# Chunked attention and Fourier mix: the first batch's scores and exponentials in halves of the queries, and a newly planned order

## The chip, the cores and the metric

The kernel runs on one core of a Trainium2 chip. The metric is the device time of one execution in microseconds; what counts is the median over runs. Five engines work in parallel, each through its own instructions in order: PE (TensorE, matrix products), DVE (VectorE), ACT (ScalarE), POOL (GpSimd) and SP (SyncE, which only issues transfers here). POOL and ACT issue transfers too. PE writes to PSUM, a small memory of eight banks of 2 KB per partition; ScalarE and VectorE read it from there.

## The reference

```python
# q, k, v: (4, 8, 768, 64); mem_k, mem_v: (4, 8, 8, 64); w_ch1: (512, 2048); w_ch2: (2048, 512)
chunk, left_ctx, right_ctx = (32, 16, 8)
for c in range(nc):                        # 24 chunks of 32 queries
    c_start = c * chunk
    c_end = c_start + chunk
    l_start = max(0, c_start - left_ctx)
    r_end = min(S, c_end + right_ctx)
    k_full = np.concatenate([mem_k, k_ctx], axis=2)      # memory and keys l_start..r_end
    v_full = np.concatenate([mem_v, v_ctx], axis=2)
    scores = scale * np.matmul(q_c, k_full.transpose(0, 1, 3, 2))
    scores = scores - np.max(scores, axis=-1, keepdims=True)
    a = np.exp(scores)
    a = a / (np.sum(a, axis=-1, keepdims=True) + 1e-09)
    out[:, :, c_start:c_end] = np.matmul(a, v_full)
# x: the heads side by side, (4, 768, 512)
X = np.fft.fft(x, axis=1)
X = np.fft.fft(X, axis=2)
u = x + np.real(X).astype(np.float32)
un = (u - mu) / np.sqrt(var + 1e-06)       # over the last axis
ch = np.maximum(un @ w_ch1, 0.0) @ w_ch2
return (u + ch).astype(np.float32)
```

## The kernel before

The work goes by batch, four in all, and in each batch by pairs of heads, four pairs (n = 0 to 15 over the kernel, n = 0 to 3 in the first batch).

**Attention of a pair.** POOL issues the loads of q and k (`e_load_qk`, L356, into three buffers each), SP those of v (`e_load_v`, L368, four buffers `va`). PE turns q and k so that the head's dimension lies on the partitions (`e_turn_q`, `e_turn_k`, both through `turn`, L389 to L394); ACT copies q (`e_qT`), DVE or ACT copies k (`e_kT`) into a window of 96 keys for each tile of 64 queries: eight memory keys and 88 of the sequence, enough for both chunks of 32 queries in the tile. The two chunks, the halves, see different keys, so the exponential is taken once for each half with its own bias column of `mbias`, which masks the others (`e_masks`, L321).

For the first eight pairs scores come in two groups g of six tiles. `e_scores` (L442) writes 12 matmuls, six tiles by two heads, to a PSUM tile `sc` of two banks, one for each head. `e_exp` (L453) reads it with two activations, one for each half. There is one such tile (`sc=1` in the plan), so the next group's scores come after both. `e_values` (L489) multiplies by v, 24 matmuls a group, and `e_norm` (L505) divides by the sum on DVE. Pairs from n = 8 take all 24 score matmuls in one go (`a_scores`, L463) with two further banks, and pairs 4 to 7 use `e_scores` with the two exponentials as separate tasks.

**After attention.** The first batch has its own Fourier stage (`first_fourier`, L1211), which works as the values of the pairs come in; the others use `fourier`. A DFT along the sequence (`g_row`, `g_rows`, `e_rows`), one along the columns (`e_columns`, `h_columns`, `e_last_row`), sums and statistics on DVE, the normalised rows on ACT (`e_un`), and the two layers (`e_ch1`, `e_relu`, `e_ch2`, `e_prod`) follow. The tables of sines and cosines are computed in the kernel's first 14 us (`e_sines`, from angles on DVE), then ACT loads the exponential table (L1191). Until the first Fourier matrices are ready, PE's free time is filled with matmuls on zeros (`e_fill`, L1002, "idle" in the profile).

**The order.** Everything is added as a task (`add`, L57) with an engine, a cost, predecessors (`after`, `behind`), buffers that it takes and gives, and a rank. `Plan.order` (L106) plays the tasks in time: whenever an engine is free, the task of lowest rank that can start is placed. The instructions are emitted in the order of placement, and that fixes each engine's queue. Waits between engines come from the tiles' accesses, not from the plan's times. Without a given rank, a task's rank is its number. A table `moved` (L1547) overrides ranks by task number; its entries are numbers from a search. `WARM` is the time up to which the plan counts PE's tasks double, `FILL` the length of a filler. Task numbers follow the order of the `add` calls: 20 and 21 are the memsets of `kTb` (L1011), 32 is DVE's second step of the D angles (L1028), 36 the turn of the memory keys (L1160), 38 to 45 the loads, turns and copies of pair 0.

Of the kernel before, what the change touches and what calls it, by code (L numbers as in the profile page):

```python
# [37 lines left out]
class Plan:  # L38
# [7 lines left out]
    WARM = 6.0  # L46
# [3 lines left out]
    FILL = 0.215  # L50
    filling, fill = None, None
# [5 lines left out]
    def add(self, engine, cost, emit, after=(), take=(), give=(), rank=None, moved=0.0,  # L57
            loose=False, late=0.0, filler=False, behind=None, lag=0.0, pick=None, grain=0.1, head=1.0, dense=0.15):
        t = dict(engine=engine, cost=cost, emit=emit, after=[a for a in after if a is not None],
                 take=take, give=give, rank=len(self.tasks) if rank is None else rank,  # L60
                 moved=moved, done=None, at=None, no=len(self.tasks), loose=loose,
                 late=late, filler=filler, behind=behind, lag=lag, picks=[pick] if pick else [], grain=grain, head=head, dense=dense)
        self.tasks.append(t)
        return t
# [41 lines left out]
    def order(self):  # L106
        now, idle = 0.0, {}
# [8 lines left out]
        while any(waiting.values()):  # L116
# [5 lines left out]
            for e, ts_ in waiting.items():  # L122
# [3 lines left out]
                for t in ts_:  # L126
# [29 lines left out]
                    cost = t["cost"] * (2.0 if e == "PE" and now < self.WARM else 1.0)  # L156
                    idle[e] = t["end"] = now + cost - (0.0 if t["moved"] else self.OVER.get(e, 0.0))
# [38 lines left out]
def kernel(  # L196
# [11 lines left out]
    nc = tc.nc  # L208
# [64 lines left out]
    plan = Plan(dict(qs=NS, ks=NS, va=NV, kTb=NKT, kU=NKU, qT=2, tr=1, sc=1, xa=1, e1=3,  # L273
# [168 lines left out]
    def e_scores(n, g):  # L442
        qT, kT = qT_of[n], kTb[n % NKT]
        sc_of[n, g] = sc = aps.tile([P, 2, 8, 64], FP32, tag="sc", bufs=1, name="sc")
        for t6 in range(6):
            t = 6 * g + t6
            for hh in range(2):
# [3 lines left out]
                                 tile_position=(r0, 0))  # L451

# [524 lines left out]
    t_table = add("ACT", 1.55, lambda: nc.scalar.activation(warm, zero, AFT.Sin), [t_zero], rank=-3)  # L977
    t_iota = add("POOL", 0.7, e_iota, rank=-5)
    t_mkf = add("ACT", 1.3, e_mkf, moved=2.04, grain=0.077)
    t_id = add("POOL", 0.7, lambda: make_identity(nc, ident), rank=-1.5)  # L980
    t_scales = add("DVE", 0.2, e_scales, [t_iota], rank=-19)
    t_ones = {}
    def e_idb():
# [5 lines left out]
    t_idb = add("DVE", 0.5, e_idb, [t_id], rank=-16.5)  # L989
    t_kz = add("DVE", 0.5, lambda: nc.vector.memset(ks[0][QP:KP], 0.0), rank=-16.95)  # L990
    t_kzs = add("POOL", 2.0, lambda: [nc.gpsimd.memset(ks[i][QP:KP], 0.0) for i in range(1, NS)],
                rank=14)
    for i in range(NV):
        e_ = add("DVE" if i < 2 else "POOL", 0.68, lambda i=i: e_edges(i),
                 rank=(-20, -17.3, 17, 17)[i])
        t_ones[i] = add("POOL", 0.7, lambda i=i: e_edge_ones(i), [e_], rank=(-3.5, 2, 17.1, 17.1)[i])
    t_masks = add("POOL", 0.86, e_masks, rank=16)
# [13 lines left out]
    t_kTz = [add("POOL", 0.45, lambda i=i: nc.gpsimd.memset(kTb[i][:, :, KEYS:P], 0.0), rank=3)  # L1011
# [8 lines left out]
    for nm, parts, y, r, NN, c in (("S", tabS, yS.rearrange(fl3), rS.rearrange(fl3), S, 1.36),  # L1020
                                   ("D", tabD, yD.rearrange(fl2), rD.rearrange(fl2), DM, 0.77)):

        t1 = [add("DVE", 0.5, lambda p_=p_: nc.vector.tensor_scalar(
            p_[0], p_[2], p_[4], FSC, ALU.mult, ALU.add), [t_scales], rank=ANG[nm] + 0.1 * i)
            for i, p_ in enumerate(parts)]
        t2 = add("DVE", 0.95 if nm == "S" else 0.6, lambda y=y, NN=NN: nc.vector.tensor_scalar(
            y, y, FSC, float(NN), ALU.subtract, ALU.mult), t1, rank=ANG[nm] + 1)
# [18 lines left out]
    def attention(n):  # L1046
# [28 lines left out]
        else:  # L1075
            tq = (add("PE", 0.46 if first else 0.56, lambda: e_turn_q(n), [lq, t_idb], take=("tr",), give=("qs",))
# [5 lines left out]
            if n in JOINED:  # L1082
                tk, ktag = tq, pick_of.setdefault(("k", n), dict(of=("mlp", "acc")))
                tk["after"] += [lq, lk]
                tk["cost"] += 0.81
# [3 lines left out]
            else:  # L1089
                tk = add("PE", 0.48 if first else 0.56, lambda: e_turn_k(n), [lk, t_idb, t_kz if n == 0 else t_kzs],  # L1090
# [6 lines left out]
        if whole:  # L1097
            sp_ = pick_of["s", n] = dict(of=("mlp", "acc"))
            s_ = add("PE", 0.52, lambda: a_scores(n), [eq, ek, t_val[n - 1]], take=("sc", "tr"), pick=sp_, give=("qT", "kTb"))
        for g in range(2):  # L1100
            if whole:
                t_used["kTb", n % NKT] = t_sc[n, g] = s_
                for part in range(2):
# [4 lines left out]
                                           give=((), ("sc",), ("tr",), (sp_,))[2 * g + part])  # L1108
                    xs_.append(x_)
            else:  # L1110
                s_ = add("PE", 0.30 if first else 0.37, lambda g=g: e_scores(n, g), [eq, ek], take=("sc",),
                         give=("qT", "kTb") if g == 1 else (),
                         behind=t_sc.get((n, 0)))
                t_used["kTb", n % NKT] = s_
                t_sc[n, g] = s_
                x_ = None
                for halves in ((0, 1),) if first else ((0,), (1,)):
                    t_exp[n, g] = x_ = add("ACT", 1.05 if first else 0.58,
# [3 lines left out]
                                           give=("sc",) if 1 in halves else ())  # L1122
# [4 lines left out]
            if not first:  # L1127
                vp = dict(of=("mlp", "acc"))
                pick_of["v", n] = vp
                v_ = t_val[n] = add("PE", 1.64, lambda: [e_values(n, i) for i in range(2)]  # L1130
                                    + [x(n + 2) for x in (e_turn_q, e_turn_k) if n + 2 in JOINED],
                         xs_ + [lv], take=("xa",), pick=vp, give=("e1", "e1", "va"))
# [7 lines left out]
            v_ = add("PE", 0.85, lambda g=g: e_values(n, g), [x_, lv], take=(tag,),  # L1140
# [50 lines left out]
    add("ACT", 1.4, lambda: nc.scalar.activation(warm, zero, AFT.Exp), [t_sines], rank=SINES)  # L1191
    t_neg = add("DVE", 0.6, e_negatives, [t_sines], rank=100)
    t_rows = add("DVE", 1.6, e_table_rows, [t_sines, t_neg], rank=101)
# [126 lines left out]
    def columns_of(b, t_rest):  # L1320
# [21 lines left out]
        def columns(kt):  # L1342
            if b > 0 and kt > 2:
                if kt == 3:
                    cols[kt] = add("PE", 0.75, lambda: e_last_row(b), [t_sum[0]])
                return
            if b >= HALVED:
                cols[kt] = add("PE", 0.58, lambda: h_columns(b, kt), allr + t_mir_ + [cols.get(kt - 1)], take=("acc",),
# [8 lines left out]
            cols[kt] = add("PE", 0.9, lambda: e_columns(b, kt),  # L1357
# [237 lines left out]
```

## Time and profile before

| what | value |
|---|---|
| median of 3 runs | 276.81 us (276.75 to 277.06) |
| the profiled execution | 276.94 us |
| its span, first to last instruction | 275.2 us |
| instructions | 8215 |
| mean granted TensorE clock | 1.000 |
| scores of groups, first batch (L449), 15.50 to 34.60 us | 96 matmuls, 2.79 us busy |
| values, first batch (L501), same stretch | 192 matmuls, 7.28 us busy |
| turns of q and k (L393), same stretch | 80 matmuls, 2.68 us busy |
| exponentials (L459), 15 to 36 us | 16 activations of 96x384, 574 ns median |
| HBM read and written | 37.36 MB, 13.37 MB |

The page's utilization by slices shows how the engines share the span; each digit is a fortieth of it, in tenths.

```profile
PE   8789999999999999999999999999999999999995
PEld 2356689898866588757758978888989888888884
DVE  7987997962336999699995999659998985354444
ACT  2675557877775278747666554838164383615150
POOL 7961365161111073016009074101000480000000
```

PE's row is full from the third slice on, but a busy PE also counts the matmuls on zeros, which the rows of the groups tell apart (`idle` on line L1005).

### The profile page before, as it was taken

How to read it: one execution, taken by the hardware profiler on the slowest of the kernel's cores; microseconds unless marked ns; L12 is line 12 of the kernel's file. 1: busy time of each engine (PE TensorE's matmuls, PEld its weight loads, DVE VectorE, ACT ScalarE, POOL GpSimd, SP SyncE). 2: the span in 40 equal slices, each digit the busy share in tenths (PEclk: the TensorE clock that was granted, in tenths of full speed). 3: DMA queues.
4: the chain of work that ended last, by engine and by line, in shares of the span. 5: the costliest groups of instructions: out<-in, count | busy, mean ns of one | idle time of the engine just before them, and what ended most of it. 6: DMA issues, size and time to landing. Idle time of an engine off the chain costs nothing.

```text
span 275.2 us, 8215 instructions
## 1 busy us (share of the span) xinstructions
PE 266.5 (97%) x3407; PEld 212.6 (77%) x3407; DVE 205.6 (75%) x460; ACT 154.9 (56%) x296; POOL 78.1 (28%) x145
## 2 busy tenths in 40 slices
PE   8789999999999999999999999999999999999995
PEld 2356689898866588757758978888989888888884
DVE  7987997962336999699995999659998985354444
ACT  2675557877775278747666554838164383615150
POOL 7961365161111073016009074101000480000000
PEclk9999999999999999999999999999999999999999
DMA  6999699999979979948999996274942106723152
GB/s 107 177 186 181 108 183 196 205 194 202 192 132 255 202 203 207 182 86 150 238 161 220 188 137 140 56 105 174 152 155 38 40 21 80 168 82 76 65 89 79
DMA packets 116118, 40.00 MB, mean 145 GB/s; under 512 B 104560, under 2 KB 111472, under 8 KB 116080
## 3 DMA queue, kind: packets, MB, share of 16 engines
q1 hardware_dynamic: 93888, 23.54, 47.4%
q0 software_dynamic: 21472, 15.21, 34.1%
q10 hardware_dynamic: 720, 0.72, 0.8%
q8 instruction: 27, 0.44, 0.7%
q14 instruction: 11, 0.09, 0.1%
HBM read 37.36 MB, written 13.37 MB: 184 GB/s over the span
## 4 chain that ended last, share of the span: by engine, by line
PE 81%; DVE 7%; POOL 6%; DMA 2%; issue 1%; ACT 1%; POOLq 0%; DVEq 0%
PE ph L881 28%; PE pc L948 16%; PE pc L899 10%; PE ps L573 6%; PE xa L501 4%; PE xo L501 4%; PE pm L743 3%; DMA qs<-in_q_dram 2%; PE ps L732 2%; PE sc L472 1%; PE trk L393 1%; PE trq L393 1%; PE sc L449 1%; DVE hT L936 1%; DVE S L936 1%
## 5 line engine op out<-in xcount | busy, mean ns | idle before, releaser
L881 PE MATMUL ph<-unT,w_sb 128*128 128x256 f16 x768 | 89.2, 273 | 0.0
L881 PEld LDWEIGHTS <-w_sb 128*128 128x128 f16 x768 | 74.0, 98 | 9.4 <-issue 0.2
L890 ACT ACTIVATE hT<-ph 128x512 f16<-128x512 f32 x96 | 56.2, 599 | 43.2 <-PE pc L948 23.3
L948 PEld LDWEIGHTS <-hT 128*128 128x128 f16 x320 | 30.9, 98 | 5.7 <-issue 1.4
L948 PE MATMUL pc<-w_sb,hT 128*128 128x256 f16 x256 | 31.9, 272 | 0.9 <-DVE xsb L953 0.9
L953 DVE TENSOR_TENSOR xsb<-pc,xsb 128x256 f32<-128x256 f32 x57 | 23.6, 420 | 11.4 <-PE pc L948 10.0
L899 PE MATMUL pc<-w_sb,hT 128*128 128x512 f16 x128 | 29.5, 380 | 0.0
L899 PEld LDWEIGHTS <-hT 128*128 128x128 f16 x128 | 11.9, 98 | 13.2 <-issue 0.2
L484 ACT ACTIVATE e<-sc,mbias 96x192 f32<-96x192 f32 (+1 forms) x48 | 18.5, 472 | 5.6 <-PE sc L472 5.6
L459 ACT ACTIVATE e<-sc,mbias 96x384 f32<-96x384 f32 x32 | 16.8, 573 | 5.6 <-PE sc L449 5.6
L936 DVE TENSOR_TENSOR S<-hT 128x768 f16<-128x768 f16 (+1 forms) x16 | 6.7, 421 | 17.7 <-ACT hT L890 17.3
L1005 PE MATMUL idle<-dz 128*128 128x512 bf16 x63 | 18.4, 423 | 1.0 <-DVE zero L311 1.0
L585 ACT CAST up<-ps 128x386 f16<-128x386 f32 x16 | 9.5, 605 | 16.6 <-PE ps L573 15.4
L816 DVE BATCH_NORM_STATS2 st<-xsb 128x6 f32<-128x512 f32 x24 | 16.4, 682 | 0.4
L411 ACT COPY qT<-trq 128x768 bf16<-128x768 bf16 x12 | 9.5, 796 | 11.3 <-PE trq L393 11.3
L948 PE MATMUL pc<-w_t,S 128*128 128x256 f16 x128 | 15.6, 273 | 0.0
L501 PEld LDWEIGHTS xa<-va,e 96*64 96x64 f32 x384 | 12.5, 137 | 3.2 <-issue 2.2
L501 PE MATMUL xa<-va,e 96*64 96x65 f32 x384 | 14.7, 226 | 0.0
L501 PE MATMUL xo<-va,e 96*64 96x65 f32 x384 | 14.1, 223 | 0.0
L365 POOL DMA_DIRECT2D qs<-in_q_dram x12 | 8.0, 670 | 19.4 <-PE trq L393 15.3
L948 PEld LDWEIGHTS <-S 128*128 128x128 f16 x128 | 12.3, 98 | 1.6 <-DVE S L936 0.2
L830 ACT ACTIVATE un<-xsb,rs 128x512 f16<-128x512 f32 x16 | 12.0, 804 | 2.7 <-POOL rs L845 2.7
(187 smaller groups left out, 477.4 us busy)
## 6 DMA issues: line engine op xcount, KB each, us to landing
va<-in_v_dram SPq DMA_DIRECT2D x32, 220.0 KB
w_sb<-in_moe_w_ch_dram POOLq DMA_DIRECT2D x8, 512.0 KB, 15.8
out_dram<-xsb SPq DMA_DIRECT2D x12, 256.0 KB
qs<-in_q_dram POOLq DMA_DIRECT2D x12, 192.0 KB, 6.1
ks<-in_k_dram POOLq DMA_DIRECT2D x12, 192.0 KB, 7.1
x_rows<-xsb POOLq DMA_DIRECT2D x3, 768.0 KB, 5.6
xr<-x_back POOLq DMA_DIRECT2D x3, 768.0 KB, 5.8
out_rows<-xsb SPq DMA_DIRECT2D x9, 256.0 KB
```

The source lines that it names most:

```text
L459: nc.scalar.activation(e1[0:KEYS, :, :, ts(half, 32)], sc[0:KEYS, :, 0:6, ts(half, 32)], AFT.Exp, bias=mbias[0:KEYS, half:half + 1], scale ...
L484: nc.scalar.activation(to, src, AFT.Exp, bias=mbias[0:KEYS, half:half + 1], scale=1.0 / math.sqrt(D))
L501: nc.tensor.matmul(xa[64 * half:64 * half + 64, st, hh, 0:65], e1[0:KEYS, hh, t6, :], v1[0:KEYS, hh, 6 * g + t6, 0:65], start=True, stop=True)
L573: nc.tensor.matmul(out_[:, sp, :], part[:, ab, sp * 3 + st, c0:c1], tab[:, sp, st, :], start=(st == 0 and i == 0), stop=(st == 2 and i == 1))
L816: nc.vector.bn_stats(st6, xs[b][:, kt, :])
L881: nc.tensor.matmul(ph[:, k, :], w1_sb[:, dt, ts(HH * k + i, P)], unT_of[b, j][:, dt, :], start=(dt == 0), stop=(dt == NDT - 1))
L890: nc.scalar.activation(hT_of[b, j][:, :, i, :], ph, AFT.Relu, bias=0.0, scale=1.0 if (b, j) in FAST else -1.0)
L899: nc.tensor.matmul(pc_of[b, j, r], hT_of[b, j][:, k, i, ts(r, P)], w2_sb[:, HH * k + i, :], start=(i + k == 0), stop=(i + k == HH))
L936: nc.vector.tensor_tensor(out_[:, lo:hi], a[:, lo:hi], c[:, lo:hi], op)
L948: nc.tensor.matmul(pc_of[key], a[:, i, :], w[:, i, :], start=(i == 0 and new), stop=(i == HH - 1), skip_group_check=not new)
L953: nc.vector.tensor_tensor(u, pc, u, ALU.add)
L1005: nc.tensor.matmul(fill_of[0], dz, strided(dz, 0, [[0, 4], [1, P]]), start=True, stop=True)
```

## The change

Three things change.

**Halves.** In the first batch, scores and exponentials go by halves. `e_half_scores` writes the scores of 32 queries of each tile, 12 matmuls of 32 columns, to one of two places in the same two banks: `[head, half, 256]`, of which 192 columns are used. `e_half_exp` reads that place. The tile is made once and kept for the first batch. The plan counts the two places as two of `sc`; everything else that uses the tile takes both.

```diff
+    def e_half_scores(n, g, half):
+        qT, kT = qT_of[n], kTb[n % NKT]
+        if "half" not in sc_of:
+            sc_of["half"] = aps.tile([P, 2, 2, 4 * 64], FP32, tag="sc", bufs=1, name="sc")
+        for t6 in range(6):
+            t = 6 * g + t6
+            for hh in range(2):
+                r0 = 64 * hh
+                nc.tensor.matmul(sc_of["half"][:, hh, half, ts(t6, 32)], kT[r0:r0 + 64, t, :],
+                                 qT[r0:r0 + 64, 64 * t + 32 * half:64 * t + 32 * half + 32],
+                                 start=True, stop=True, tile_position=(r0, 0))
+
+    def e_half_exp(n, g, half):
+        if half == 0:
+            e1_of[n, g] = apool.tile([P, 2, 6, 64], FP32, tag="e1", bufs=3, name="e1")
+        nc.scalar.activation(e1_of[n, g][0:KEYS, :, :, ts(half, 32)],
+                             sc_of["half"][0:KEYS, :, half, 0:192].rearrange("p h (t q) -> p h t q", t=6),
+                             AFT.Exp, bias=mbias[0:KEYS, half:half + 1], scale=1.0 / math.sqrt(D))
...
+                for half in range(2) if first else ():
+                    s_ = add("PE", 0.30, mode="s", emit=lambda g=g, half=half: e_half_scores(n, g, half), after=[eq, ek], take=("sc",),
+                             give=("qT", "kTb") if (g, half) == (1, 1) else (), behind=t_sc.get(n))
+                    t_used["kTb", n % NKT] = t_sc[n] = s_
+                    t_exp[n, g] = x_ = add("ACT", 0.58, lambda g=g, half=half: e_half_exp(n, g, half),
+                                           [s_, t_masks, x_], take=() if half else ("e1",), give=("sc",))
```

**What the planner counts.** A PE task has a mode ("s" for scores and the last row, "v" for turns and values, none for the rest), and going from none to a mode costs `TURN`. A slot `port` is taken by most of the DVE and POOL tasks of the first 15 us, so that the plan lets only one of them run at a time. `WARM` goes from 6.0 to 4.5, and many costs are set anew. None of this emits an instruction; it changes the order.

```diff
-    WARM = 6.0
+    WARM = 4.5
+    TURN = 0.106
...
+                    if e == "PE":
+                        cost += self.TURN if t["mode"] and not mode and now < idle.get(e, 0.0) + 0.05 else 0.0
+                        mode = t["mode"]
...
-    plan = Plan(dict(qs=NS, ks=NS, va=NV, kTb=NKT, kU=NKU, qT=2, tr=1, sc=1, xa=1, e1=3,
+    plan = Plan(dict(qs=NS, ks=NS, va=NV, kTb=NKT, kU=NKU, qT=2, tr=1, sc=2, port=1, xa=1, e1=3,
...
+    def shared(t):
+        t["take"] += ("port",)
+        t["give"] += ("port",)
+        return t
+
+    t_id = shared(add("POOL", 0.6, lambda: make_identity(nc, ident), rank=-1.5))
...
+    t_kzs = shared(add("POOL", 1.6, lambda: [nc.gpsimd.memset(ks[i][QP:KP], 0.0) for i in range(1, NS)],
+                rank=14))
...
-            s_ = add("PE", 0.52, lambda: a_scores(n), [eq, ek, t_val[n - 1]], take=("sc", "tr"), pick=sp_, give=("qT", "kTb"))
+            s_ = add("PE", 0.456, mode="s", emit=lambda: a_scores(n), after= [eq, ek, t_val[n - 1]], take=("sc", "sc", "tr"), pick=sp_, give=("qT", "kTb"))
...
-                v_ = t_val[n] = add("PE", 1.64, lambda: [e_values(n, i) for i in range(2)]
+                v_ = t_val[n] = add("PE", 1.551, mode="v", emit=lambda: [e_values(n, i) for i in range(2)]
```

**The ranks.** All entries of `moved` are replaced. The first of each:

```diff
-        2: -18.38, 10: -9.99, 13: 4.81, 14: 260.95, 15: 4.82, 34: -8.71, 38: -60.89, 71: 16.24,
...
+        20: -365.43, 32: 282.14, 36: 226.88, 59: 287.72, 100: 117.58, 142: 301.34, 143: -324.8,
+        147: 235.85, 150: 497.72, 160: 383.83, 165: 261.67, 174: 390.21, 180: 318.66, 250: 125.95,
...
```

A first-batch pair has four tasks more than before (two score groups and two exponentials as separate tasks), so numbers from pair 0's scores on shift; 59 is now the k load of pair 1 and 100 the v load of pair 3.

More of the change, by code (lines that the diff above doesn't have):

```diff
@@ L57, in add @@
     def add(self, engine, cost, emit, after=(), take=(), give=(), rank=None, moved=0.0,
[L58 removed]
+            loose=False, late=0.0, filler=False, behind=None, lag=0.0, pick=None, grain=0.1, head=1.0, dense=0.15, mode=""):
         t = dict(engine=engine, cost=cost, emit=emit, after=[a for a in after if a is not None],
@@ L61, in add @@
                  moved=moved, done=None, at=None, no=len(self.tasks), loose=loose,
-                 late=late, filler=filler, behind=behind, lag=lag, picks=[pick] if pick else [], grain=grain, head=head, dense=dense)
+                 late=late, filler=filler, behind=behind, lag=lag, picks=[pick] if pick else [], grain=grain, head=head, dense=dense, mode=mode)
         self.tasks.append(t)
@@ L106, in order @@
     def order(self):
-        now, idle = 0.0, {}
+        now, idle, mode = 0.0, {}, ""
         self.flow, self.seen, self.clear = {}, 0.0, 0.0
@@ L1075, in attention @@
         else:
-            tq = (add("PE", 0.46 if first else 0.56, lambda: e_turn_q(n), [lq, t_idb], take=("tr",), give=("qs",))
+            tq = (add("PE", 0.463, mode="v", emit=lambda: e_turn_q(n), after=[lq, t_idb], take=("tr",), give=("qs",))
                   if n not in JOINED else t_val[n - 2])
```

68 lines of the change are left out of this document (32 added, 36 removed), and 20 rows, old and new, of the table moved.

## The prediction

> **What bounds it now.** I read the page's busy table and chain first, then the chain in order of time, the order of PE's instructions up to 62 us, the waits, and busy time by stage.
>
> ```profile
> PE 266.5 (97%) x3407; PEld 212.6 (77%) x3407; DVE 205.6 (75%) x460; ACT 154.9 (56%) x296; POOL 78.1 (28%) x145
> ...
> L1005 PE MATMUL idle<-dz 128*128 128x512 bf16 x63 | 18.4, 423 | 1.0 <-DVE zero L311 1.0
> ```
>
> The 97% misleads: 63 of PE's matmuls (18.4 us) are the idle fillers of L1005. By stage:
>
> ```profile
> 6.50:15.50 9.00, 5.96 (x68) 2.88 (x68) 8.80 (x19) 6.26 (x9) 8.40 (x21) 1.00 1.18 179
> 15.50:34.60 19.10, 18.68 (x398) 12.30 (x399) 15.93 (x41) 11.20 (x25) 6.29 (x18) 1.00 1.00 154
> 34.60:54.70 20.10, 19.97 (x279) 17.14 (x278) 17.73 (x40) 14.38 (x28) 9.71 (x17) 1.00 1.07 196
> 54.70:272.10 217.40, 216.47 (x2652) 178.41 (x2649) 158.06 (x345) 121.62 (x234) 48.64 (x78) 1.00 0.79 140
> ```
>
> After the length come busy PE, PEld, DVE, ACT, POOL, then clock, DMA share, GB/s. All fillers lie before 34.6 us. After that PE works on the result and stands still for 0.13 + 0.93 us until 272.1, then 3.1 us of tail. So the kernel is a lead-in of 34.6 us, 237.5 us of PE work, and a tail. It shortens if the lead-in does, or if that PE work does. The lead-in's chain:
>
> ```profile
> 13.14 1.99 POOL ks L991 x2
> ...
> 15.92 0.65 POOL ks L365
> ...
> 17.36 6.62 DMA qs<-in_q_dram
> 24.03 0.53 PE trq L393 x16
> ...
> 29.07 0.28 PE sc L449 x12
> 29.35 0.85 PE xo L501 x24
> 30.20 0.75 PE idle L1005 x3
> 30.96 0.28 PE sc L449 x12
> 31.24 0.32 PE idle L1005
> 31.56 0.87 PE xa L501 x24
> 32.46 0.21 DVE zs L511
> ```
>
> POOL's late loads, then rounds of scores (0.28), exponentials and values, with fillers between. In PE's order the eight scores start at 15.53, 18.22, 20.02, 22.12, 25.21, 27.02, 29.00 and 30.89: seven rounds of 2.19 us. ScalarE's two exponentials for a round:
>
> ```profile
> 15.98 1.04 ACT L459 ACTIVATE e<-sc,mbias 96x384 f32<-96x384 f32 x2 [0.69 <-PE sc L449]
> ...
> 18.61 1.04 ACT L459 ACTIVATE e<-sc,mbias 96x384 f32<-96x384 f32 x2 [0.91 <-PE sc L449]
> ```
>
> **Part 1, halves.** Eight score groups of 12 matmuls become sixteen, over 32 query columns instead of 64. No row has that shape. Each still loads its own weights (12 loads of 95 ns, overlapped), so a group costs between half of 0.28 and all of it; I take 0.28, as 64 columns already pass in 23 ns each and 193 columns in 85. That adds 8 x 0.28 = 2.2 us to PE (0 to 2.2). The cover is the fillers: 30 after 15.5 us, some 6.5 us at 216 ns each. Without it, all 2.2 would show. The exponentials stay sixteen of 96x384 at 574 ns: no change.
>
> The unknown is whether one half's scores may be written while ScalarE reads the other half, in the same two banks. No row of before shows PE writing a bank that another engine reads. From above: they overlap. A round then costs what PE does in it: 0.56 scores + 0.79 values + 0.30 turns (five turns of 0.47 left after 15.5, over eight rounds) = 1.65, a gain of 0.54 each, 3.8 over seven. DVE is close behind: its 15.93 of 19.10 allows 3.2. From below: they wait. Then it matters how the order emits them. Where both halves stand next to each other on PE before either exponential, a round is 0.56 + 0.17 (last score's end to the exponential: 15.88 to 15.98, and the 0.07 by which the pipelined end exceeds the issue) + 1.04 + some 0.2 back = 1.97 us. The 0.2 is an estimate: exponential to next score is 0.32 at least (26.70 to 27.02) with fillers in it. Gain 0.22 a round, 1.5 in all. Where they alternate, the round is 2 x (0.28 + 0.17 + 0.57 + 0.2) = 2.44: a loss of 0.25 each, 1.8 in all, and the values and turns queued behind the blocked score on PE wait too, with the normalisation on DVE behind them.
>
> I take waiting with adjacent halves: -1.5. PE has about 1.65 us of work per round against 1.05 of ScalarE, so a values block usually stands between pairs; when it ends, the planner has both places free and emits the two halves together. The Trainium skill (PSUM — Partial Sum Buffer, "PSUM bank collisions raise a hardware error") says that two engines may not touch one bank in the same partitions at once, even at different addresses, and that one should guard by bank. It speaks against the change's second place: by it the round is 1.97 at best, by the free overlap 1.65; no run here shows which yet.
>
> **Part 2, lead-in order.** By the new ranks and the port slot, I follow POOL's list through its first ten us. The k-padding memset (task 20, -365) goes first and pair 1's k load (task 59, 287.72) goes after the kU memsets; the memsets that share the port fall behind while DVE holds it, so the four DMA issues of pairs 2 and 3 come before the 2.0 us of L991, instead of 12.45, 15.92, 17.36 and 18.00. That removes the 6.62 us piece of the chain, which made two of the seven rounds long (2.69 and 3.09), so the round above is reachable. It costs q of pair 0 some 1.2 us (one memset and the iota now ahead of it). Its turn was at 7.98, waiting for the identity, so this is covered unless the identity is early. The v loads on SP keep their place but share the DMA, 1.18 busy, with these loads; v was gated at 26.40 and its values needed at 31.49, five us of cover. DVE's step for the D angles (task 32, 282.14) falls behind the key copies; its sine stood at 12.33 and the exponential table behind it ends at 15.29, so a delay of 0 to 1 us would move the first exponential from 15.98 directly. Against that, the S angles are no longer held up by POOL. I take 0, with -0.5 to +1.0.
>
> **Part 3, the order after 45 us.** The planner now charges 0.106 for turning PE to another matmul mode. The chain shows it: a block of eight behind attention, and one among its own kind:
>
> ```profile
> 107.89 0.98 PE ph L881 x8
> ...
> 168.94 0.87 PE ph L881 x8
> ```
>
> Counting entries from plain matmuls into L393, L449, L472, L501 and L624 in PE's order after 45 us gives 27, some 2.9 us. Scores are tied to exponentials and values, so only part can be put side by side: 0 to 12 (the whole-score groups), 1.3 us. I take 4: -0.4. The refined lengths only change the order; PE's real work is the same. What new stalls or cured ones it brings, the trace cannot show: before has 0.93 us to cure, and a stall like the 0.60 at 164.41 on DVE could come a few times. I take 0, with -0.7 to +2.5.
>
> **Sum.** -1.5 + 0 - 0.4 + 0 = -1.9. The profiled execution took 276.94 (span 275.2 and 1.74 around it), the median of the runs is 276.81. From 276.94 this gives 275.0, beside the median 274.9.
>
> **Rivals.**
> 1. The halves truly overlap: -3.2 (DVE's room) - 0.4 = 273.3. For: different addresses, ScalarE idle 5.0 us behind the scores. Against: one bank. Also holds if the planner saves more turns.
> 2. Alternating halves block PE (slower). A score of one half is emitted behind the other half's exponential; each waits for it. Round 2.44: +1.8 + values late in the last round (0.8) - 0.4 = 279.0. It decides when the mean round exceeds 2.19. For: the planner believes the places independent, so whenever PE is idle it emits singly. Against: PE is fuller than ScalarE.
> 3. The new order stalls after 34.6 us: the halves gain 1.5 but PE, DVE or a load is late in the crowded part, at +2.5 to +4: 278.0. For: DMA is busy (1.07) from 34.6 to 54.7, and the first layer's weights, issued at 39.33 with a median 15.8 us to landing, are wanted at 54.68. Against: no PE wait over 0.6 there now.
> 4. The change does nothing, because those weights land at the same time anyway: lead-in gain eaten at 54.68, about 276.5.
>
> **Numbers.** Forecast 0.34, rival 1 0.20, rival 2 0.17, rival 3 0.19, rival 4 0.10. A difference of 0.2% (0.55 us) is about what this kernel's runs can tell from none. Faster: 0.34 + 0.20 + 0.02 from rival 4 = 0.56; same: 0.07 of rival 4; slower: 0.17 + 0.19 + 0.01 = 0.37. The likeliest case alone spans 273.8 (start 0.5 earlier, 0.7 cured) to 276.2 (start 1.0 late, no turns saved). The range, with both signs, is 271.9 (rival 1 with 12 turns saved and 0.5 at the start) to 279.4 (rival 2 with a little of 3).
>
> **What will show it.** The score starts give the round: 1.65, 1.97 or 2.44. A wait of PE's score on the exponential, or scores that run while one does, tell waiting from overlap. POOL's issue times of pairs 2 and 3 should fall below 12 us. The first filler-free us should come near 33, the count of mode entries near 23, and PE's idle time after it stay below 2 us. I am wrong if the rounds shorten and the time does not, or if weights or values become PE's wait.

## The result, and the profile after

The changed kernel takes 279.97 us in the median of four runs (278.77 to 280.20), the kernel before beside it 276.94 (276.75 to 277.12). The ratio is 1.0101, with a 95% interval of 1.0070 to 1.0132: about 3 us slower, where 274.9 was forecast, and above the range's high end of 279.4. The profiled execution took 280.18 us (span 278.5). Medians here and below are of all runs, while a ratio leaves out the runs that took over 1.5% more than the fastest of their kernel.

The same parts of the page as before: PE's busy line, the row of the fillers, and the stages, the second of which now ends where the first Fourier matmul starts, at 37.50 us (34.60 before).

```profile
PE 268.2 (96%) x3500; PEld 214.9 (77%) x3500; DVE 204.8 (74%) x460; ACT 155.1 (56%) x296; POOL 77.3 (28%) x145
...
L1033 PE MATMUL idle<-dz 128*128 128x512 bf16 x60 | 18.3, 443 | 1.0 <-DVE zero L315 1.0
```

```profile
6.50:15.50 9.00, 6.84 (x69) 3.11 (x66) 8.16 (x19) 5.35 (x8) 7.77 (x18) 0.81 1.31 205
15.50:37.50 22.00, 19.58 (x493) 14.15 (x492) 15.85 (x42) 12.80 (x28) 5.13 (x23) 1.00 0.79 140
37.50:54.70 17.20, 17.20 (x242) 14.67 (x240) 14.84 (x34) 11.89 (x22) 8.95 (x15) 1.00 1.03 189
54.70:275.33 220.63, 219.15 (x2688) 180.88 (x2686) 160.21 (x351) 123.58 (x237) 49.56 (x78) 1.00 0.81 140
```

Nearly the whole loss stands ahead of 37.50: the lead-in is 2.90 us longer, and the profiled execution 3.24. The stretch from 37.50 to 275.33 is 237.8 us (237.5 before); PE is idle for 1.48 us of it where the rows before show 1.06, and the tail is 3.2 us (3.1 before). The granted clock of the lead-in's first stage is 0.81: from 12 to 14 us it is half. And the 22.00 us of its second hold 19.58 of PE's work, so PE stands still for 2.42 us in the middle of the attention (0.42 before).

The chain in order of time over the lead-in answers to the chain shown of before:

```profile
10.46 0.15 DVE ident_b L1012
...
18.54 1.83 PE idle L1033 x8
20.38 0.27 PE sc L465 x12
...
20.66 0.59 ACT e L472
...
21.29 0.33 PE sc L465 x12
...
21.65 0.59 ACT e L472
...
24.45 0.48 PE sc L465 x24
...
25.02 1.05 ACT e L472 x2
```

POOL's loads and their 6.62 us piece are gone from it. In their place it begins with the identity, and holds two kinds of group. Where a line says x24 and x2, both halves stand together: one round of 1.66 us. Where it says x12, then one exponential, then x12, they alternate. ScalarE's and PE's own rows show the waits:

```profile
17.15 1.03 ACT L472 ACTIVATE e<-sc,mbias 96x384 f32<-96x384 f32 x2
20.66 0.58 ACT L472 ACTIVATE e<-sc,mbias 96x384 f32<-96x384 f32 x1 [2.49 <-PE sc L465]
21.65 0.58 ACT L472 ACTIVATE e<-sc,mbias 96x384 f32<-96x384 f32 x1 [0.41 <-PE sc L465]
...
25.02 1.05 ACT L472 ACTIVATE e<-sc,mbias 96x384 f32<-96x384 f32 x2 [0.61 <-PE sc L465]
```

```profile
10.65 0.53 PE L397 MATMUL trq<-ident_b,qs 96*64 96x96 bf16 x16 [2.16 <-DVE ident_b L1012]
...
27.78 0.47 PE L465 MATMUL sc<-qT,kTb 64*128 64x32 bf16 x24 [0.35 <-ACT e L472]
```

The first exponential comes at 17.15 us (15.98 before), the eight groups' exponentials at 17.15, 20.66, 23.36, 25.02, 26.68, 28.34, 31.81 and 33.32. A round goes from one of them to the next; below it is named by the group in which it ends, the second to the eighth. Four rounds take 1.66 us or less, but the second takes 3.51, the third 2.70 and the seventh 3.47; the mean is 2.31 (2.19 before). So the 2.90 us are 1.17 of a later first exponential, 0.81 in seven rounds, and 0.92 behind the start of the eighth group's, whose second half starts only at 34.30. This counts where the time lies, not what causes it: the chain does not pass through the first exponential, but through PE's fillers to the second group's scores.

### The profile page after: what moved, and what is told of

Same layout as the page of the kernel before. It is cut to its first block, busy times and chain, and to the rows that moved or that the text cites. A ratio compares the mean times of both kernels' runs of the same rounds, so it can differ in the third digit from the quotient of the medians.

```text
span 278.5 us, 8407 instructions
## 1 busy us (share of the span) xinstructions
PE 268.2 (96%) x3500; PEld 214.9 (77%) x3500; DVE 204.8 (74%) x460; ACT 155.1 (56%) x296; POOL 77.3 (28%) x145
## 4 chain that ended last, share of the span: by engine, by line
PE 86%; DVE 10%; ACT 1%; issue 1%; ACTq 0%
PE ph L904 30%; PE pc L971 16%; PE pc L922 10%; PE ps L596 6%; PE xa L524 4%; PE xo L524 3%; PE ps L755 3%; PE idle L1033 3%; PE pm L766 2%; PE trk L397 2%; PE trq L397 2%; DVE st L839 1%; PE sc L495 1%; ACT e L472 1%; DVE yS L1051 1%
## 5 line engine op out<-in xcount | busy, mean ns | idle before, releaser
L971 PE MATMUL pc<-w_sb,hT 128*128 128x256 f16 x256 | 32.1, 273 | 0.5 <-DVE xsb L976 0.4
L959 DVE TENSOR_TENSOR S<-hT 128x768 f16<-128x768 f16 (+1 forms) x16 | 7.4, 462 | 20.7 <-ACT hT L913 20.3
L534 DVE RECIPROCAL zs<-xa 128x6 f32<-128x6 f32 x16 | 3.0, 189 | 18.8 <-PE xa L524 18.8
L853 ACT ACTIVATE un<-xsb,rs 128x512 f16<-128x512 f32 x16 | 12.8, 816 | 6.8 <-POOL rs L868 6.8
L827 POOL TENSOR_TENSOR xsb<-mix,xr 128x512 f32<-128x512 f32 x6 | 8.1, 1361 | 25.0 <-ACT mix L821 23.8
```

The costliest lines, as they stand in the source:

```text
L853: nc.scalar.activation(un, xs[b][:, kt, :], AFT.Identity, bias=rs[:, 1:2], scale=rs[:, 0:1])
L971: nc.tensor.matmul(pc_of[key], a[:, i, :], w[:, i, :], start=(i == 0 and new), stop=(i == HH - 1), skip_group_check=not new)
```

## The experiments

Five theories were tested. **Theory 1**: PE's queue is late from the start, by the late identity, the clock that falls to half in that wait, and fillers that stand ahead of work that is ready. **Theory 2**: the halves wait for one another in their shared banks, and cost what that adds. **Theory 3**: the turn of pair 3's q, at 28.93 us, is late. **Theory 4**: PE runs short of instructions, as its stream is 192 matmuls and weight loads longer ahead of 35 us; **4b**: PE's queue holds ready scores behind other work. **Theory 5** came out of the sixth and seventh run: a load of values is late once the lead-in is early. "First Fourier" below is the start of that matmul in the profiled run. It is one execution for each kernel: in the change, c_whole, d_pairs and p_after_v4, which have the same order up to there, the first exponential alone came between 17.14 and 17.75 us, so differences below some 0.6 us say little. Each run has the kernel before beside it on the same chip (median 277.19 to 277.46).

The edits of order act on the list from which the instructions are emitted, by task number; `ahead` and `behind` move one task next to another. 46 to 49 and 52 to 55 are pair 0's scores and exponentials by halves, and so on for the other pairs; 103 and 104 are the turn and copy of pair 3's q, 233 and 250 the loads of the values of pairs 4 and 5.

### The identity first: a_identity

```diff
-        for t in plan.settled(moved):
+        order = plan.settled(moved)
+        ahead(order, 4, 34)
+        ahead(order, 6, 29)
+        for t in order:
             t["emit"]()
```

> The changed kernel with POOL's identity and DVE's copies of it emitted earlier (the identity ahead of the kU memsets, the copies ahead of the S angles' last step); all else in its order. Theory 1 (PE's queue is late: the turn of pair 0 waits for the identity until 10.65 us, the 2.2 us without work let the clock fall to half until about 15.4, and the fillers that stand in PE's order ahead of the second group's scores then run late): first turn below 9 us, no stretch at clock 0.5, second group's scores by 18.6 instead of 20.31, time 1.5 to 2.0 us under the changed kernel's 279.97. Theory 2 (the loss is the scores of one half waiting for the exponential of the other): the waits stay, so does the time, within 0.5 us. Theory 3 (the loss is the late turn of pair 3's q, 28.93 us): within 0.5 us as well, as that turn's place is untouched.

Measured: 283.31 us, ratio 1.0220 (1.0194 to 1.0247), slower than the change. The first turn came at 9.14 instead of 10.65, so the identity was what held it. The first exponential came at 15.49 instead of 17.15, though the scores for it had been ready since 13: ScalarE's sines ahead of it began 2.37 us sooner, as DVE's first three steps of the S angles took 1.10 us instead of 2.96. But POOL's load of pair 2's q slid from 7.51 to 9.03 us. PE's weight loads of the edited kernel:

```profile
16.06 0.40 PEld L397 LDWEIGHTS <-qs 96*64 96x64 bf16 x16 [3.06 <-DMA qs<-in_q_dram]
```

PE's queue is in order, so all of it stood behind this turn for 2.76 us, the clock was half from 16.6 to 20.0 us, and the second group's scores came at 21.67 instead of 20.31. The clock was half again from 37.1 to 40.5 us, over the last values and fillers. First Fourier: 40.34. The expected gain missed; what it showed is that the loads are spaced tightly behind the identity, and that a stretch at half speed followed this wait of PE too.

### Ten more fillers ahead of the first turn: b_fillers

```diff
+        at = next(i for i, o in enumerate(order) if o.get("no") == 42)
+        order[at:at] = [dict(emit=e_fill)] * 10
```

> The changed kernel with ten more fillers on PE ahead of the first turn, which fill its gap of 2.2 us; nothing else moves. Theory 1, the clock's part alone: the first turn stays near 10.7, the clock stays at 1.00, the scores of pair 0 come some 1.5 us sooner than 15.50, the second group's by 18.8, time 1.0 to 1.8 under 279.97, and the runs agree more closely than the changed kernel's 278.77 to 280.2. Theories 2 and 3: no change beyond 0.3 us.

Measured: 279.81 us, ratio 1.0100 (1.0068 to 1.0132). The clock stayed at 1.00 from 8 to 18 us, the first scores came at 14.05 instead of 15.50, but the first exponential at 17.27: it waits for the table load of 1.28 us on ScalarE, which stands behind the sines. First Fourier 36.19, 1.31 earlier than in the change. The median hardly follows (279.97 to 279.81, intervals that overlap). Theory 1's clock loss is real and worth 1.3 us in that profile. But not every execution of the change has it: of its four runs, two show a mean clock of 0.993 (280.18 and 280.20 us), two of 1.000 and 0.999 (279.76 and 278.77), and these are slower than the kernel before as well.

### The change's order with whole scores: c_whole

```diff
-emit=lambda g=g, half=half: e_half_scores(n, g, half)
+emit=lambda g=g, half=half: e_scores(n, g) if half == 0 else None
...
-lambda g=g, half=half: e_half_exp(n, g, half)
+lambda g=g, half=half: e_exp(n, g, (half,))
```

> The changed kernel's order with the halves undone: the scores of a group are written in one go of 12 matmuls of 64 columns at the place of its first half, and nothing at the place of the second. Theory 2: most of the loss goes, time 277 to 277.7. Theories 1 and 3: the order carries the loss, time 279.0 to 280.0; at most 1.0 us goes with the waits inside the groups that alternate (second group of pair 0, second group of pair 3).

Measured: 278.51 us in ten runs (276.58 to 282.11), ratio 1.0048 (1.0017 to 1.0078). First Fourier 34.95, 2.55 earlier than in the change, with the same order of everything else. ScalarE's rows here:

```profile
25.24 1.05 ACT L482 ACTIVATE e<-sc,mbias 96x384 f32<-96x384 f32 x2 [0.50 <-PE sc L453]
26.79 1.05 ACT L482 ACTIVATE e<-sc,mbias 96x384 f32<-96x384 f32 x2 [0.50 <-PE sc L453]
```

A round of whole scores takes 1.55 us in this order, with one place, where a round of adjacent halves takes 1.66. The order alone leaves the lead-in 0.35 longer than before. The median lies between what theory 2 expected (277 to 277.7) and theories 1 and 3 (279.0 to 280.0): the halves carry the larger part of the loss, the order the rest.

### Halves alone, in the order of before: h_halves

Both halves are emitted next to each other in the place of the whole group.

```diff
-lambda g=g: e_scores(n, g)
+lambda g=g: [e_half_scores(n, g, half) for half in range(2)] if first else e_scores(n, g)
...
-lambda g=g, halves=halves: e_exp(n, g, halves)
+lambda g=g, halves=halves: [e_half_exp(n, g, half) for half in halves] if first else e_exp(n, g, halves)
```

> The kernel before, in its own order, with only the scores in halves: both halves of a group one behind the other (24 matmuls of 32 columns, two places), then both exponentials. Theory 1 and 3: the halves cost only PE time, 0.40 instead of 0.28 us a group, inside the stretch with fillers: within 0.5 us of 276.94. Theory 2: the two places in one bank cost time of their own, 0.25 a round or more, 278.5 or above.

Measured: 280.22 us (278.46 to 281.33), ratio 1.0120 (1.0067 to 1.0173); first Fourier 36.89, 2.29 later than before. In the order of before, 1.78 us of it are one stall inside a block of values:

```profile
26.84 0.34 PE L520 MATMUL xo<-va,e 96*64 96x65 f32 x5 [1.78 <-issue]
```

"issue" means that the profile shows nothing that PE waited for. The place is PE's 705th matmul or weight load. The trace has 16 KB packets on the queue that carries instructions; one ran from 23.91 to 25.35 us, and PE went on 1.49 us after its end. The halves themselves cost the other 0.5 us here.

### All halves adjacent: d_pairs

```diff
+        for first_, second_ in ((52, 54), (66, 68), (72, 74), (86, 88), (92, 94), (107, 109), (113, 115)):
+            behind(order, second_, first_)
```

> The changed kernel with the two halves of each group put directly one behind the other on PE (the second half's scores moved up to the first's, ahead of the first half's exponential); nothing else moves. Theory 2 (the halves that alternate wait for each other in the shared bank): the two alternating groups (second of pair 0, second of pair 3) and the one split by a turn (first of pair 1) fall from 2.0 to 2.7 us a round to 1.7, values of pair 3 come 0.9 earlier, the first Fourier matmul at 35.6 to 36.2 instead of 37.5, time 278.2 to 279.0. Theory 1 (the clock and the late identity alone): unchanged, 279.5 to 280.2.

Measured: 280.62 us (278.98 to 282.68), ratio 1.0117 (1.0060 to 1.0174). First Fourier 35.79, 1.71 earlier than in the change: that is what the two alternating groups cost, with the one whose halves a turn splits (the third round fell from 2.70 to 1.62 us), as theory 2 says. The lead-in therefore adds up over profiles that differ by one thing each: 34.60 before, +0.35 for the order (c_whole), +0.84 for adjacent halves (d_pairs against c_whole), +1.71 for alternating ones (the change against d_pairs) is 37.50. The first two are near the scatter of single profiles; counted from the second group's exponential on, the adjacent halves cost 0.58. But the profiled run took 282.68, more than the change. Something behind the lead-in took back more than was won.

### Whole scores, fillers and an early third turn: k_whole_fill_turn

c_whole with the ten fillers of b_fillers, and the third turn of q behind the second pair's scores:

```diff
+        behind(order, 103, 74)
+        behind(order, 104, 75)
```

> The changed kernel's order with whole scores in place of the halves, the ten fillers ahead of the first turn, and pair 3's q turned right behind pair 1's last scores (its copy on ScalarE behind pair 1's last exponential) instead of behind pair 1's values. Theory 3 (the late turn of pair 3 makes the seventh round 3.4 us long): all rounds after the second near 1.6, first Fourier matmul near 32, 276.9 - 2.5 = 274.4 (273.8 to 275.5), faster than both kernels. If the turn is not what holds the seventh round: first Fourier matmul at 33.6, time 276 to 276.7.

Measured: 277.78 us in ten runs, spread from 276.25 to 283.25; ratio 1.0001 (0.9965 to 1.0036). The turn moved to 22.38 us, and still pair 3's scores came at 28.43: they stand behind two blocks of pair 2's values, and the seventh round is 3.16 us (3.35 in c_whole). So theory 3 falls, and 4b takes its place. First Fourier 33.70, 0.90 ahead of the kernel before, in an execution of 282.02 us. PE's rows in that execution, and SP's:

```profile
62.15 0.34 PE L524 MATMUL xa<-va,e 96*64 96x65 f32 x4
66.35 0.80 PE L524 MATMUL xa<-va,e 96*64 96x65 f32 x20 [3.87 <-DMA va<-in_mem_v_dram]
```

```profile
36.75 0.59 SPq L382 DMA_DIRECT2D va<-in_v_dram  x1
...
42.06 11.28 SPq L378 DMA_DIRECT2D va<-in_v_dram  x2
53.39 0.32 SPq L387 DMA_DIRECT2D va<-in_mem_v_dram  x1
```

The first values that the second batch multiplies are those of pair 4. The change's order has SP load pairs 5 and 6 first, then 4; before, 4 came first, at 21.56 to 26.99 us. In k_whole_fill_turn it is handed over from 36.75 to 53.71, since two issues hold SP for 11.28 us: POOL's loads of the layers' weights, from 35.97 on, fill the transfer engines. From 44 to 60 us POOL's queue moved 2.68 MB and SP's 0.48, in about as many packets (2,009 and 1,927). The Trainium skill (DMA: Bandwidth & Descriptors, "Queues, rings and completion order") says that each transfer engine takes the queues in turn, a packet at a time. Equal packets with unequal bytes agree with that, as POOL's are 1 and 4 KB and those of v 256 bytes; whether the page counts the same unit as a packet, no run here shows. After 3.87 us of waiting PE's clock was half from 67 to 71 us. In the change the same load was handed over at 37.58 to 40.84 and used at 65.96 without a wait, because the lead-in was late. This is theory 5. The four of the ten runs above 280 us show a mean clock of 0.988 to 0.994, the other six of 0.998 to 1.000.

### The same with halves: l_fill_pairs_turn

b_fillers, d_pairs and the third turn together.

> The same with the halves kept and put in pairs: fillers, pairs and the earlier turn. Against the whole scores it costs 0.12 of PE and of waiting in each of eight rounds: 0.9 us slower than the run with whole scores, 275.3 (274.6 to 276.5). If the halves overlapped with the exponentials anywhere, it would be the faster of the two.

Measured: 280.92 us (279.58 to 284.12), ratio 1.0108 (1.0050 to 1.0167). That is 3.1 us above k_whole_fill_turn, where 0.9 was expected. First Fourier 34.33, so the lead-in was 3.17 us shorter than in the change; the wait for pair 4's values was 4.34 us, in an execution of 284.12. By the start of the first Fourier matmul the profiles with the change's order of loads show a wait of 0 at 37.50 and 36.19 (b_fillers), 2.40 at 35.79 (d_pairs), 0 at 34.95 (c_whole), 4.34 at 34.33 and 3.87 at 33.70: an early start brings it in most of them, not in all.

### More instructions without halves: j_split_fillers

The kernel before, with each filler as two matmuls of 256 columns: the same work in more instructions.

```diff
+        for part in range(2):
+            nc.tensor.matmul(fill_of[0][:, ts(part, 256)], dz, strided(dz, 0, [[0, 2], [1, P]]),
+                             start=True, stop=True)
```

> The kernel before with each filler of 512 columns written as two of 256: the same PE time, twice the filler instructions, some 80 more instructions on PE by 24 us, about as many as the halves bring by then. Theory 4 (in the run with only the halves PE stood 1.8 us inside a block of values, at its 705th matmul or weight load, 1.5 us after the end of a 16 KB transfer on the instruction queue: PE ran out of instructions): a stall of 1 to 2 us without a releaser near 24 to 26 us here too, at about that count, time 278 to 280. If that stall came from the halves or the values' load: no stall, time within 0.3 us of 276.94.

Measured: 278.77 us in ten runs (276.90 to 281.85), ratio 1.0045 (1.0019 to 1.0071). PE stood for 0.69 us on "issue" at its 705th matmul or weight load again, from 24.82 to 25.50. A longer stream alone makes the kernel slower and its runs uneven: theory 4 holds as a second price of the halves, though the profile of the change itself has no such stall, and it is no part of its 2.90 us. No row names what is late there; the last section has what the traces show of it.

### The late load first: n_whole_v4

k_whole_fill_turn with one edit more:

```diff
+        ahead(order, 233, 250)
```

> Whole scores, ten more fillers and the early turn of pair 3's q (the edits of k_whole_fill_turn) and, new, on SP's queue the load of the first values that the second batch uses (pair 4) ahead of those of pairs 5 and 6, where the kernel before has it. In k_whole_fill_turn the first Fourier matmul came at 33.70 us, .9 ahead of the kernel before, and still its profiled run took 282.0: PE waited 3.87 us for that load at 62.5 to 66.35 and the clock fell after it. Theory 5 (late load): SP hands that load over last of three, from 36.75 to 53.71 us, in the flood of POOL's weight loads, so that an earlier end of the lead-in finds nothing to work on; with it first no wait at 62 us is left, the loss after the lead-in goes, and the time is the kernel before's less .9, near 276 us, in all runs alike (the spread of 276.3 to 283.3 goes too). Rival (the transfers are at their limit anyway): the wait moves to pair 5 or to the weights, at 62 to 75 us, and the time stays at 278 or above.

Measured: 276.82 us in twelve runs, 276.35 to 277.83; the kernel before 277.46; ratio 0.9974 (0.9958 to 0.9989). PE's row at the place of the wait:

```profile
62.52 0.92 PE L524 MATMUL xa<-va,e 96*64 96x65 f32 x24
```

All 24 matmuls in one piece, no wait, and the spread of 7.0 us has become 1.5; the mean clock is 0.999 or 1.000 in all twelve runs. Theory 5 is shown by the one edit; its rival, that another transfer takes the wait over, is not seen. The gain on the kernel before is 0.6 us of the 0.9 expected; its first Fourier came at 34.06 in this profile, 0.54 ahead of the kernel before.

### Pair 3's scores ahead of pair 2's values: o_whole_v4_s3

```diff
+        ahead(order, 107, 90)
+        ahead(order, 109, 90)
```

> The same with, in addition, pair 3's first scores ahead of pair 2's two blocks of values on PE: in k_whole_fill_turn they start at 28.43 us though the exponential before them ended at 26.78, behind 1.7 us of those blocks and a filler. Theory 4b (order of PE's queue): the seventh round falls from 3.16 to near 1.6 us, the first Fourier matmul comes near 32.1 to 32.5, 2 us ahead of the kernel before, and the time is near 274.5 to 275 us. Rival (DVE's preparation of the Fourier sums, or the transfers, hold the start or take it back): the first Fourier matmul comes early but the end stays at 276, with PE waiting at 36 to 75 us.

Measured: 276.21 us in nine runs (275.65 to 277.10), ratio 0.9951 (0.9932 to 0.9970): faster than the kernel before by 0.5% and, by the two ratios, than the changed one by some 1.5%. The seventh round fell to 1.54 us (exponentials at 25.72 and 27.26), but the eighth rose to 2.60, behind those same blocks and three fillers; first Fourier at 33.12, not 32.1 to 32.5. Part of what was won was given back one round later; 4b holds with a smaller size. Of the 1.48 us by which this first Fourier is ahead of the kernel before, 0.8 reaches the end of the span (274.4 against 275.2). The rival's wait at 36 to 75 us is not there (0.21 at most), so where the rest goes stays open.

### The halves in the mended order: q_pairs_v4_s3

o_whole_v4_s3 with the change's halves, adjacent.

> The same as o_whole_v4_s3 with the change's halves, both halves of a group next to one another on PE. It prices the halves with the identity's clock loss, the queue's order, the third turn and the late load all taken out. Theory 2 (halves add PE work and wait for the same banks, nothing more): eight rounds of 1.66 instead of 1.57 us and 0.1 us of extra matmuls, .5 to 1 us above o_whole_v4_s3. Rival (halves cost more, through PE's instruction stream, which is 192 instructions longer ahead of 35 us): 2 us or more above o_whole_v4_s3, with a stall of PE that waits for nothing in 24 to 36 us.

Measured: 277.99 us in twelve runs, ratio 1.0045 (1.0012 to 1.0079), 1.8 us above o_whole_v4_s3. The runs lie in two groups, eight from 277.13 to 278.67 and four from 280.63 to 281.22; the profiled one, 280.87, is of the upper group. Its PE and a window of its clock (the third number from the end):

```profile
25.82 0.26 PE L465 MATMUL sc<-qT,kTb 64*128 64x32 bf16 x7 [0.83 <-issue]
```

```profile
28.00:30.00 2.00, 2.00 (x44) 1.45 (x42) 1.53 (x4) 0.91 (x2) 1.74 (x4) 0.50 0.96 201
```

The stall is at the 705th matmul or weight load once more, and behind it the clock is half from 27.5 to 34.3 us; first Fourier 38.19. Both expectations hold a part: the middle of the lower group, 277.7, is 1.5 us above o_whole_v4_s3, where theory 2 had 0.5 to 1, and the profiled run of the upper group has the stall that the rival named. The upper group's four runs have a mean clock of 0.982 to 0.988, the lower group's eight of 0.998 to 1.000, so the lower group lacks the half speed; whether it lacks the stall too was not profiled.

### The load alone: p_after_v4

The change with only `ahead(order, 233, 250)`.

> The changed kernel with one edit: the load of pair 4's values ahead of those of pairs 5 and 6 on SP. In the changed kernel's profile PE does not wait for it at 65.96 us, since the lead-in ended 2.9 us late. Theory 5 and theory 1 together: the profiled time stays near 280 us, first Fourier matmul still near 37.5, since the load only binds once the lead-in is early; at most the runs come closer together. Rival (the load's place is the whole of the loss): the time falls to 277.

Measured: 280.13 us (280.07 to 280.96), ratio 1.0095 (1.0074 to 1.0117); first Fourier 37.44. The load's place is not the loss of the change. It decided only what could be won back.

## Why the prediction was wrong

The step that failed is in part 1: "Gain 0.22 a round, 1.5 in all". The halves were priced right, or too high; what they were subtracted from was wrong. I set an adjacent round of 1.97 against the mean of 2.19. But that mean was not the price of a whole-score round with one place. It held rounds of 2.69 and 3.09 and others behind fillers and blocks. Part 2 puts both long ones down to the 6.62 us load, but that load ends at 24.03: only the second round holds a wait for it, of 0.38 us, and the first holds eight fillers. In an order that lets the rounds run, whole scores take 1.55 us (c_whole) and adjacent halves 1.66. The halves had nothing to gain: with them the lead-in is 0.84 longer where they stand together, 1.71 more by the two groups where they alternate. The term measures +2.55 in this order instead of -1.5, and in the order of before +0.5 and a stall of 1.78. The times agree: with the halves taken out, the change's order runs 1.5 us faster (c_whole), and the mended order 1.8 (o_whole_v4_s3 against q_pairs_v4_s3).

Point by point:

**The unknown of the bank** came out as taken: they wait. No score of one half ran beside an exponential of the other; six waits of PE on ScalarE, 0.29 to 0.45 us each. The Trainium skill's rule (PSUM — Partial Sum Buffer, "PSUM bank collisions raise a hardware error") is that one guards by bank and not by address, and the waits in the traces do so: they guard the whole tile. What an access without them would do, no run here shows. Rival 1 is out.

**The matmuls** of 32 columns were taken at 0.28 us for twelve and measured at 0.40 for the pair of groups, 0.20 each, so adjacent rounds were 1.66, better than 1.97. The added PE time lies under the fillers, as said.

**"The planner has both places free and emits the two halves together"** was right for six groups of eight. The two others are rival 2 ("each waits for it"), with the mechanism named there and a chance of 0.17. Its time of 279.0 is the nearest to what was measured; its condition, a mean round above 2.19, was met at 2.31. That the time is so near is in part luck: rival 2 took all rounds as alternating, at a loss of 0.25 each, 1.8 in all. Here two groups alternated, and with the one split by a turn they cost 1.71; the clock loss of the late identity is no part of rival 2.

**Part 2: "I take 0".** POOL's issues of pairs 2 and 3 came at 7.51, 9.03, 11.49 and 12.13 us instead of 12.45, 15.92, 17.36 and 18.00, as foretold. The price was not 0, in two places.

On PE, "covered unless the identity is early" assumed that the identity keeps its time. It came at 8.16 to 9.03 on POOL instead of 5.83 to 7.31, between the first two of these issues, so the first turn came at 10.65 instead of 7.98 and the clock halved behind the wait, which b_fillers prices at 1.31 us.

On ScalarE, the first exponential came 1.17 us later, beyond the bound of +1.0, and by the step that the prediction names. DVE's task 32 ended at 14.24 instead of 12.29, so the D sine and, behind it, the exponential's table came some 2 us later. The first two rows are of before, the others of the change:

```profile
12.33 0.63 ACT L1173 ACTIVATE sinD<-tri 128x512 f16<-128x512 f32 x1 [0.22 <-DVE tri L1028]
13.79 1.28 ACT L1191 ACT_TABLE_LOAD   x1
```

```profile
14.37 0.63 ACT L1206 ACTIVATE sinD<-tri 128x512 f16<-128x512 f32 x1
15.74 1.28 ACT L1224 ACT_TABLE_LOAD   x1
```

It is not the clock's work: in b_fillers, with full clock and the scores at 14.05, the exponential came at 17.27. Nor did "the S angles are no longer held up by POOL" hold: DVE's first three steps of them took 2.96 us, where they took 2.41 before and 1.10 in a_identity.

"The round above is reachable" did not hold for all rounds either: eight fillers ahead of the second group, and two blocks of values ahead of the seventh, made two rounds of 3.5.

**Part 3** held in its count, not in its gain: 24 mode entries after 45 us against 27 (23 foretold), and PE idle for 1.48 us behind the lead-in (below 2). But the stretch is 237.8 us against 237.5, where -0.4 was forecast: PE's work fell by 0.09 and its idle time rose by 0.42. Rival 3 did not come in the change. It came in its repairs, as the load of pair 4's values, which no step of mine had followed: I wrote that "the v loads on SP keep their place".

**Rival 4** named the wrong transfer. The weights of the layers were never waited for; in the repairs it was their crowding out of SP's small loads that set the end.

## What to carry to other kernels

Before a wait is priced, look for the shortest round of its kind in the trace, not the mean: the mean holds what other work put in, and a repair is only worth the difference to the shortest. Two places in one tile and its banks were one place to the waits here, and splitting work over them added instructions and alternation without overlap. When a stage is made shorter, follow the order of each queue's loads to the next stage's first use, since an order that was harmless behind a late stage becomes the new end.

## What was not expected of the hardware

PE's clock fell to half after short waits. It was idle from 8.49 to 10.65 us in the change, and half speed stood from 11.7 to 15.1 us; the Trainium skill (TensorE: Matmul & The Clock Gate, "HAM oscillation — how this bites in real kernels") warns of idle gaps beyond some 3.4 us, and here 2.16 was enough. In q_pairs_v4_s3 one stall of 0.83 us, among smaller waits, came ahead of 6.8 us at half speed, while h_halves kept its full clock through 1.78 us.

The clock records of the traces go some way to part them. In all 14 the granted clock changes only on a grid of 3.41 us, so that the change's half speed is one step of it and q_pairs_v4_s3's two. Counted by these steps, each of the nine that held 1.67 us or more of idle PE was followed by a step at half speed (2.16 us in the change, 2.76 in a_identity). The 1.78 us of h_halves fell into two steps, where idle time came to 0.43 and 1.35, and none followed. But idle time is not the whole rule: half speed also followed steps with 1.14 (q_pairs_v4_s3) and 0.91 us (a_identity, from 33.6 us), and none followed one with 1.58 (h_halves, from 5.0 us).

PE can stand without waiting for anything that the profile names: 1.78, 0.69 and 0.83 us in three kernels of different order, each time behind the 705th matmul or weight load of its stream, at 24.8 to 25.1 us. All 14 traces have a 16 KB packet on the instruction queue (q8) between 21 and 26.2 us, and in none does the 706th start sooner than 1.41 us after that packet's end. In the three stalls it starts 1.46 to 1.60 us after. In d_pairs and l_fill_pairs_turn it starts 1.41 and 1.51 us after, with gaps of 0.08 and 0.21 us from start to start. In the other nine PE comes there later by itself, 1.67 to 2.63 us after, and nothing stands. So instructions that land late fit every profile, and a longer stream would stall because PE gets there sooner. The change escapes as it is late: its 705th starts at 27.03 us (27.14 in the kernel before). Halves that alternate in the order of before were not tried.
